# Attention and a token/channel mixer on one core: a relu of the weight narrowing put behind a copy of ys on ACT

## The chip, the cores and the metric

One NeuronCore of a Trainium2 chip runs the whole kernel in one launch. The metric is the device time of an execution in microseconds; lower is better. PE is the tensor engine (PEld its weight loads), DVE the vector engine, ACT the scalar engine, POOL the GpSimd engine, SP the engine that issues most DMAs. SPq, ACTq and so on are the engines' sequencers.

## The reference

```python
def _attn_ref(q, k, v):                      # (8, 8, 576, 64) each: batch, head, position, d
    q_s = softmax of q over d;  k_s = softmax of k over the 576 positions
    kv = np.einsum('bhsd,bhse->bhde', k_s, v)
    return np.einsum('bhsd,bhde->bhse', q_s, kv)

def reference(...):
    x = attn.transpose(0, 2, 1, 3).reshape(8, 576, 512)
    h = np.maximum(x.transpose(0, 2, 1) @ w_tok1, 0.0) @ w_tok2     # 576 -> 256 -> 576, over positions
    u = x + h.transpose(0, 2, 1)
    return u + np.maximum(u @ w_ch1, 0.0) @ w_ch2                   # 512 -> 1536 -> 512, over channels
```

The softmaxes are written out here in words. q, k and v come as fp32, the four weights as 64-bit floats.

## The kernel before, in words

**The units.** The attention and the token mixing are cut into 32 units of two heads each (128 channels by 576 positions). A unit goes through these stages: `softmax_k` (DVE maximum, ACT exponential `kt_t`) and `softmax_q` (DVE reductions and multiplications around an ACT exponential of `q_t`); `stage_qT` and `stage_kv` on PE (transposes of q and k through PSUM, the product `kvf` of k and v with its scale `rs`); `stage_y` (PE: q by w_tok1, then ACT copies the result out of PSUM as `ys`, L424); `stage_h1` (PE L430: `ys` by `kvf`, ACT relu to `hh`, DVE remainder to `hl`); `stage_u` (PE L464: `hh` and `hl` by w_tok2, added to the attention product; ACT casts the result to `uh`, DVE L472 writes the remainder `ul`). The pair hh/hl, uh/ul and so on is the high and low part of an fp32 number; products are taken as three passes of parts. The first 8 units are "early": they run while the weights are still being brought in. The other 24 run later, between the channel products.

**The weights.** A weight arrives as pairs of 32-bit words. `narrow` makes fp32 out of it in five DVE operations (L234, L236, L237, L239, L241) with one ACT relu (L235) behind the first of them; `split` then writes the high part with an ACT cast (L134) and the low part with a DVE subtraction (L135). `load_tok2` brings w_tok2 in this way as two pieces of 512 columns (n = 0 and 1) and a tail of 128. In the order lists cv_s_281 is the piece n = 1, ys_266 the ys of unit 0 and ys_359 that of unit 1.

**The rest.** The channel mixing runs over 9 groups of 512 positions: L487 makes a hidden block, L490 (ACT) and L491 (DVE) its relu in two parts `h`, L694 multiplies them by w_ch2. Groups 0 to 2 are done so, up to about 280 us. Meanwhile `keep_blocks` and `keep_sums` prepare sums of pairs of w_ch1 blocks for the groups after them: for each pair p, SP loads `whole` into the buffer stg (L516), DVE makes four sums (L518 to L521), ACT casts them (L134), DVE writes the remainder, and SP stores both to DRAM (L524, w<-stg). stg has two buffers, which every pair uses in turn. The groups 3 to 6 and then the last two together use these sums in a scheme of seven products per block pair.

**The order.** The program is written unit by unit, but a scheduler sets the order of each engine from a simulated timeline, so the written place of an instruction doesn't fix its place. Each engine takes its instructions strictly in the order that the scheduler wrote, and waits at the head of its line. `behind(list)` adds a constraint: instructions issued in its block come after the listed ones in the engine's order.

Of the kernel before, what the change touches and what calls it, by code (L numbers as in the profile page):

```python
# [11 lines left out]
AF = mybir.ActivationFunctionType  # L12
# [8 lines left out]
def attn_mixer_kernel(ctx: ExitStack, tc: tile.TileContext, q, k, kt, v, wt, out, dims):  # L21
# [3 lines left out]
    nc = tc.nc  # L25
    B, H, S, D, TOK, DM, DCH, wide = dims
# [47 lines left out]
    ebias = const.tile([P, 1], F32, name="ebias")  # L74
# [54 lines left out]
    def f32(ap):  # L129
        return ap.bitcast(F32)  # L130

    def split(hi, lo, src, lo_eng):

        nc.scalar.copy(hi, src)  # L134
        lo_eng.tensor_tensor(lo, src, f32(hi), op=ALU.subtract)  # L135
# [3 lines left out]
    def ps_unit(dtype=F32):  # L139

        pools = unit_banks[0]
        pool, name = pools[turn[0] % len(pools)]
        turn[0] += 1
        return pool.tile([P, 512], dtype, name=name)
# [7 lines left out]
    @contextmanager  # L152
    def behind(instructions):
        with ExitStack() as stack:
            for ins in instructions:
                stack.enter_context(tc.issue_after(ins))
            yield
# [32 lines left out]
    def load_weights(i, n=CW, out=None):  # L190

        if not wide:
            t = out if out is not None else cv.tile([P, C1 * P], F32, name="cv_s")[:, 0:n]
            nc.sync.dma_start(t, wt[i][:, 0:n])
            return t
        conv.append(conv.pop(0))
        raw = raw_tile(conv[-1][0])
        nc.sync.dma_start(raw[:, 0:n, :].rearrange("p n w -> p (n w)"), wt[i][:, 0:n].bitcast(U32))
        with behind(first):
            return narrow(raw, n, out)  # L200

    wide_pools = []
    spare = []

    def raw_tile(pool):
        if pool is not None:
            return pool.tile([P, CW, 2], U32, name="stg")
        if not spare:
            t = wide_pools[0].tile([P, 2 * CW, 2], U32, name="stg_w")
            spare.extend((t[:, 0:CW], t[:, CW : 2 * CW]))  # L210
        spare.append(spare.pop(0))
        return spare[-1]

    def load_wide(i, out=None):

        if not wide:
            t = out if out is not None else wide_pools[1].tile([P, 2 * CW], F32, name="cv_w")
            for x in range(2):
                nc.sync.dma_start(t[:, x * CW : (x + 1) * CW], wt[i + x])
            return t  # L220
        raw = wide_pools[0].tile([P, 2 * CW, 2], U32, name="stg_w")
        flat = raw.rearrange("p n w -> p (n w)")
        for x in range(2):
            nc.sync.dma_start(flat[:, x * 2 * CW : (x + 1) * 2 * CW], wt[i + x].bitcast(U32))
        with behind(first):
            return narrow(raw, 2 * CW, out, wide_pools[1].tile([P, 2 * CW], U32, name="cv_w"))

    def narrow(raw, n, out, s=None):


        w0, w1 = raw[:, 0:n, 0], raw[:, 0:n, 1]
        if s is None:
            s = conv[-1][1].tile([P, C1 * P], U32, name="cv_s")[:, 0:n]
        nc.vector.tensor_scalar(s, w1, 20, 0x7FF, op0=ALU.logical_shift_right, op1=ALU.bitwise_and)  # L234
        nc.scalar.activation(s, s, AF.Relu, bias=ebias, scale=2.0**23)  # L235
        nc.vector.scalar_tensor_tensor(s, w1, 0x80000000, s, op0=ALU.bitwise_and, op1=ALU.bitwise_or)  # L236
        nc.vector.tensor_scalar(w1, w1, 0xFFFFF, 0x100000, op0=ALU.bitwise_and, op1=ALU.bitwise_or)  # L237
        f1 = w1.bitcast(F32)
        nc.vector.scalar_tensor_tensor(f1, w0, 2.0**-32, w1, op0=ALU.mult, op1=ALU.add)  # L239
        z = s.bitcast(F32) if out is None else out  # L240
        nc.vector.tensor_tensor(z, f1, s.bitcast(F32), op=ALU.mult)  # L241
        return z
# [22 lines left out]
    def load_tok2():  # L265
        if WIDE2:
            t = load_wide(AT_T2).rearrange("p (n s) -> p n s", n=NT)
            split(w2h[:, :, 0:S0], w2l[:, :, 0:S0], t, nc.vector)
        else:
            for n in range(NT):  # L270
                split(w2h[:, n, 0:S0], w2l[:, n, 0:S0], load_weights(AT_T2 + n), nc.vector)
        t = load_weights(AT_TAIL + 1, NT * TL).rearrange("p (n t) -> p n t", n=NT)
        split(w2h[:, :, S0:S], w2l[:, :, S0:S], t, nc.vector)

    whole = {}

# [134 lines left out]
    def stage_y(u):  # L411
        y = ps_unit()
        if u["early"]:
            mm = [(u["q"][:, c, :], w1f[:, c, :]) for c in range(C1)]
        else:
            qh, ql = u["qh"], u["ql"]
            mm = []
            for c in range(C):
                mm += [(qh[:, c, :], w1h[:, c, :]), (qh[:, c, :], w1l[:, c, :]), (ql[:, c, :], w1h[:, c, :])]
            mm += [(qh[:, C, :], w1th), (qh[:, C, :], w1tl)]  # L420
        for i, (a, w) in enumerate(mm):
            nc.tensor.matmul(y[:, 0:TOK], a, w, start=(i == 0), stop=(i == len(mm) - 1))  # L422
        ys = (early if u["early"] else wk).tile([P, TOK], F32, name="ys")
        nc.scalar.copy(ys, y[:, 0:TOK])  # L424
        u["y"] = ys

    def stage_h1(u):
# [480 lines left out]
    units = {}  # L908
# [10 lines left out]
    def pe_stages(n):  # L919
        def s1():  # L920
            stage_qT(units[n])
            stage_kv(units[n])

        def s2():
            stage_y(units[n])

        def s3():
            stage_h1(units[n])

        def s4():  # L930
            stage_u(units[n], 0)

        def s5():
            stage_u(units[n], 1)

        return s1, s2, s3, s4, s5
# [27 lines left out]
    stages[0][1]()  # L964
    load_v(1)
    load_tok2()
    conv[:] = [(stg, cv)]
    for n in range(NE):
# [194 lines left out]
```

## Time and profile before

| what | us |
|---|---|
| median of three runs | 794.77 |
| the three runs | 794.04, 794.77, 797.56 |
| the profiled execution | 796.62 |
| its span | 794.8 |
| granted clock of PE, mean | 0.998 |
| busy: PE, PEld, DVE, ACT, POOL | 769.0, 670.9, 618.1, 341.9, 180.7 |

The profiled execution is one run of its own; it lies 1.85 above the median of the three, and 1.82 of its time lie outside the span. Busy times add up what an engine does; where two instructions of one engine overlap, the shorter of the stretches counts. In a timeline a row gives start and duration in us, the engine, the line, what it writes and reads, the shape, how many instructions the row holds, and in brackets the idle time before it and what ended that. Line numbers are those of the kernel before; the changed kernel's are 1 higher from L235 on and 3 higher from L276 on.

### The profile page before, as it was taken

The numbers are of one execution on the slowest core, as the hardware profiler recorded it, in microseconds if no ns is written. First come the engines' busy times: TensorE is split into PE (matmuls) and PEld (weight loads), VectorE is DVE, ScalarE is ACT, GpSimd is POOL, SyncE is SP. The second block draws the span as 40 slices with busy tenths as digits, with TensorE's granted clock in tenths as the row PEclk, the third lists the DMA queues.
The fourth block names the chain that finished last, engine by engine and source line by source line (L and its number), as shares of the span: only waits on it lengthen the run. The fifth ranks groups of instructions, "written<-read, shape, count | busy, mean of one in ns | idle before, by whom it ended". The sixth has DMA issues, their size and how long they took to land.

```text
span 794.8 us, 13455 instructions
## 1 busy us (share of the span) xinstructions
PE 769.0 (97%) x4824; PEld 670.9 (84%) x4824; DVE 618.1 (78%) x1101; ACT 341.9 (43%) x744; POOL 180.7 (23%) x130
## 2 busy tenths in 40 slices
PE   3899999999999999999999999999999999999998
PEld 2688888877888888899999999989999998888886
DVE  7979998978788874878688657888987557667971
ACT  4666433444454443434353334434444324346610
POOL 0000000011111352122211111232422320536640
PEclk9999999999999999999999999999999999999999
DMA  9655644158879785587879777999978543667776
GB/s 304 187 174 166 224 150 171 44 171 278 273 243 336 232 286 177 144 282 210 238 213 287 226 219 216 288 339 314 316 233 270 161 134 115 195 189 198 192 207 196
DMA packets 151459, 174.83 MB, mean 220 GB/s; under 512 B 51297, under 2 KB 98017, under 8 KB 151393
## 3 DMA queue, kind: packets, MB, share of 16 engines
q1 hardware_dynamic: 145056, 161.65, 67.2%
q10 hardware_dynamic: 6336, 12.32, 4.1%
q8 instruction: 38, 0.62, 0.3%
q14 instruction: 29, 0.23, 0.1%
HBM read 131.47 MB, written 42.47 MB: 219 GB/s over the span
## 4 chain that ended last, share of the span: by engine, by line
PE 70%; DVE 11%; issue 7%; DMA 7%; ACT 2%; POOL 1%; SPq 1%; DVEq 0%; POOLq 0%; ACTq 0%
PE ps_o L694 20%; PE ps_h L645 14%; PE ps_h L768 7%; PE ps_o L768 7%; PE ps_h L464 6%; PE ps_h L422 4%; PE ps_h L487 4%; PE ps_h L357 2%; DMA q_t<-in_q 2%; DMA stg<-whole 1%; PE ps_h L430 1%; PE ps_o L464 1%; PE ps_o L882 1%; DMA w<-stg 1%; DVE q_t L340 1%
## 5 line engine op out<-in xcount | busy, mean ns | idle before, releaser
L694 PE MATMUL ps_o<-h,c2h 128*128 128x512 f32 x544 | 184.2, 398 | 2.9 <-ACT h L490 1.9
L694 PEld LDWEIGHTS ps_o<-h,c2h 128*128 128x128 f32 x544 | 101.4, 188 | 23.8 <-ACT h L490 3.0
L694 PE MATMUL ps_o<-h,c2l 128*128 128x512 f32 x272 | 106.0, 393 | 0.0
L318 POOL TENSOR_TENSOR k_t<-k_t,dg 128x640 f32<-128x640 f32 x24 | 41.6, 1735 | 217.6 <-ACT dg L317 182.1
L135 POOL TENSOR_TENSOR ql<-q_t,qh 128x640 fp32r<-128x640 f32 x24 | 38.4, 1599 | 182.3 <-PE ps_o L694 104.2
L645 PE MATMUL ps_h<-th,ring 128*128 128x256 f32 x384 | 72.3, 283 | 0.0
L645 PEld LDWEIGHTS ps_h<-th,ring 128*128 128x128 f32 x384 | 60.1, 191 | 0.0
L694 PEld LDWEIGHTS ps_o<-h,c2l 128*128 128x128 f32 x272 | 51.3, 188 | 8.6
L487 PE MATMUL ps_h<-uh,c1l 128*128 128x512 f32 x144 | 56.2, 390 | 0.0
L487 PE MATMUL ps_h<-ul,c1h 128*128 128x512 f32 x144 | 56.2, 390 | 0.0
L487 PE MATMUL ps_h<-uh,c1h 128*128 128x512 f32 x144 | 56.1, 392 | 0.0
L645 PE MATMUL ps_h<-uh,ring 128*128 128x256 f32 x288 | 54.4, 282 | 0.6 <-DVE c L672 0.6
L645 PE MATMUL ps_h<-tl,ring 128*128 128x256 f32 x192 | 54.3, 283 | 0.0
L645 PEld LDWEIGHTS ps_h<-uh,ring 128*128 128x128 f32 x288 | 46.5, 190 | 2.8 <-DVE c L672 0.8
L471 ACT CAST uh<-ps_h 128x320 fp32r<-128x320 f32 (+4 forms) x76 | 24.4, 334 | 52.1 <-PE ps_h L464 32.1
L336 ACT ACTIVATE q_t<-q_t 128x640 f32<-128x640 f32 x32 | 23.6, 738 | 46.1 <-DVE q_t L327 43.1
L326 DVE TENSOR_REDUCE st<-q_t 128x10 f32<-128x640 f32 x32 | 26.1, 815 | 22.2 <-DMA q_t<-in_q 22.2
L490 ACT ACTIVATE h<-ps_h 128x512 fp32r<-128x512 f32 x36 | 21.5, 598 | 49.5 <-PE ps_h L487 42.0
L645 PE MATMUL ps_h<-ul,ring 128*128 128x256 f32 x144 | 40.6, 282 | 0.0
L645 PEld LDWEIGHTS ps_h<-tl,ring 128*128 128x128 f32 x192 | 36.8, 192 | 0.0
L472 DVE TENSOR_TENSOR ul<-ps_h,uh 128x320 fp32r<-128x320 f32 (+4 forms) x76 | 27.4, 370 | 9.0 <-ACT uh L471 8.8
L135 DVE TENSOR_TENSOR qtl<-q_t,qth 128x512 fp32r<-128x512 f32 (+1 forms) x48 | 25.6, 566 | 8.1 <-ACT qth L134 7.3
(319 smaller groups left out, 2070.2 us busy)
## 6 DMA issues: line engine op xcount, KB each, us to landing
ring<-w SPq DMA_DIRECT2D x210, 256.0 KB, 3.7
ring<-v SPq DMA_DIRECT2D x42, 256.0 KB, 3.0
kt_t<-in_kt SPq DMA_DIRECT2D x32, 320.0 KB, 3.7
q_t<-in_q SPq DMA_DIRECT2D x32, 320.0 KB, 3.7
v_t<-in_v SPq DMA_DIRECT2D x32, 320.0 KB, 4.5
stg_w<-in_w SPq DMA_DIRECT2D x18, 512.0 KB, 6.0
k_t<-in_k SPq DMA_DIRECT2D x24, 320.0 KB, 4.9
q<-cv_s SPq DMA_DIRECT2D x24, 320.0 KB, 3.2
```

The lines of the kernel that those rows point to most:

```text
L135: lo_eng.tensor_tensor(lo, src, f32(hi), op=ALU.subtract)
L318: nc.gpsimd.tensor_tensor(kx, kx, dg.unsqueeze(1).broadcast_to([P, C1, P]), op=ALU.subtract)
L326: nc.vector.tensor_reduce(st[:, 0, :], qt, axis=AX.X, op=ALU.max)
L336: nc.scalar.activation(qc, qc, AF.Exp)
L422: nc.tensor.matmul(y[:, 0:TOK], a, w, start=(i == 0), stop=(i == len(mm) - 1))
L464: nc.tensor.matmul(t[:, 0:N], a, w, start=(i == 0), stop=(i == len(mm) - 1))
L471: nc.scalar.copy(uh, src).ins,
L472: nc.vector.tensor_tensor(ul, src, f32(uh), op=ALU.subtract).ins,
L487: nc.tensor.matmul(t, a[:, n, :], w, start=(i == 0), stop=(i == 3 * NJ - 1))
L645: nc.tensor.matmul(t[:, cols], a, b[:, n], start=(i == 0), stop=(i == 5))
L694: m = nc.tensor.matmul(o, a[:, cs], w, start=(first and i == 0), stop=(last and i == 2))
L768: nc.tensor.matmul(o, a, b, start=first and i == 0 and (n == 0 or not one), stop=last and i == 2 and (n == 1 or not one))
```

## The change

`stage_y` keeps the instruction of the ys copy in the unit. While the second piece of w_tok2 (n = 1) and its tail are narrowed, the list `copied` holds the copy of unit 0, and the relu of `narrow` is issued behind it. For n = 0 and for all other weights the list is empty, and nothing is constrained.

```diff
-    spare = []
+    spare, copied = [], []
...
-        nc.scalar.activation(s, s, AF.Relu, bias=ebias, scale=2.0**23)
+        with behind(copied):
+            nc.scalar.activation(s, s, AF.Relu, bias=ebias, scale=2.0**23)
...
             for n in range(NT):
+                copied[:] = [units[0]["ys"]] if n else []
                 split(w2h[:, n, 0:S0], w2l[:, n, 0:S0], load_weights(AT_T2 + n), nc.vector)
         t = load_weights(AT_TAIL + 1, NT * TL).rearrange("p (n t) -> p n t", n=NT)
         split(w2h[:, :, S0:S], w2l[:, :, S0:S], t, nc.vector)
+        copied.clear()
...
-        nc.scalar.copy(ys, y[:, 0:TOK])
+        u["ys"] = nc.scalar.copy(ys, y[:, 0:TOK]).ins
```

The scheduler answers this with other choices behind it. No instruction is added or removed. Rows that differ run on PE from about row 49 to 850 of 3,200, on DVE from 68 to 400, on ACT from 25 to 260 and on SP from 29 to 97; POOL's list is the same, and so is everything from about 280 us on. Three places follow.

**First place: ACT in the head (about 28 to 32 us).** Before:

```order
L134 CAST w2h_104<-cv_s_270 128x512
L235 ACTIVATE cv_s_281<-cv_s_281,ebias_96 128x512
L424 COPY ys_266<-ps_h_260 128x256
L424 COPY ys_359<-ps_h_353 128x256
L303 ACTIVATE kt_t_390<-kt_t_390,mc_395 128x640
L437 ACTIVATE hh_364<-ps_o_361 128x256
L367 ACTIVATE kvf1_147<-ps_o_336,rs_348 64x64 x2
L303 ACTIVATE kt_t_480<-kt_t_480,mc_485 128x640
```

Now:

```order
L134 CAST w2h_104<-cv_s_270 128x512
L427 COPY ys_266<-ps_h_260 128x256
L236 ACTIVATE cv_s_281<-cv_s_281,ebias_96 128x512
L427 COPY ys_359<-ps_h_353 128x256
L306 ACTIVATE kt_t_390<-kt_t_390,mc_395 128x640
L440 ACTIVATE hh_364<-ps_o_361 128x256
L370 ACTIVATE kvf1_147<-ps_o_336,rs_348 64x64 x2
L306 ACTIVATE kt_t_480<-kt_t_480,mc_485 128x640
```

The relu of cv_s_281 and the copy of ys_266 have traded places; what stands behind them is the same.

**Second place: DVE at the softmax of the last early units (about 52 to 60 us).** st_820 and q_t_804 belong to the softmax of q of the last early unit, whose q is the transfer that DVE waits for there; the ul rows free the PSUM banks that PE writes next. Before:

```order
L472 TENSOR_TENSOR ul0_124<-ps_o_378,uh0_123 128x192
L326 TENSOR_REDUCE st_820<-q_t_804 128x10
L337 TENSOR_REDUCE st_704<-q_t_688 128x10
L327 TENSOR_TENSOR q_t_804<-q_t_804,st_820 128x640
L299 TENSOR_REDUCE mc_807<-kt_t_802 128x1
L472 TENSOR_TENSOR ul0_124<-ps_h_468,uh0_123 128x192
L472 TENSOR_TENSOR ul1_126<-ps_o_378,uh1_125 128x64
L472 TENSOR_TENSOR ul0_124<-ps_h_548,uh0_123 128x320
L338 TENSOR_SCALAR st_704<-st_704 128x10
L472 TENSOR_TENSOR ul0_124<-ps_o_558,uh0_123 128x192
```

Now:

```order
L475 TENSOR_TENSOR ul0_124<-ps_o_378,uh0_123 128x192
L340 TENSOR_REDUCE st_704<-q_t_688 128x10
L329 TENSOR_REDUCE st_820<-q_t_804 128x10
L341 TENSOR_SCALAR st_704<-st_704 128x10
L475 TENSOR_TENSOR ul0_124<-ps_h_468,uh0_123 128x192
L475 TENSOR_TENSOR ul1_126<-ps_o_378,uh1_125 128x64
L302 TENSOR_REDUCE mc_807<-kt_t_802 128x1
L475 TENSOR_TENSOR ul0_124<-ps_h_548,uh0_123 128x320
L475 TENSOR_TENSOR ul0_124<-ps_o_558,uh0_123 128x192
L330 TENSOR_TENSOR q_t_804<-q_t_804,st_820 128x640
```

Two of the ul rows now come ahead of the subtraction L330 and the maximum L302, and the sum reduction of st_704 ahead of the maximum that waits. A little further down on DVE stands hl_661, which PE needs for the next unit. Before:

```order
L234 TENSOR_SCALAR cv_w_573<-stg_w_570 128x1024
L234 TENSOR_SCALAR cv_w_587<-stg_w_584 128x1024
L338 TENSOR_SCALAR st_820<-st_820 128x10
L340 TENSOR_TENSOR q_t_688<-q_t_688,st_704 128x640
L438 SCALAR_TENSOR_TENSOR hl_661<-ps_h_657,hh_660 128x256
```

Now:

```order
L234 TENSOR_SCALAR cv_w_573<-stg_w_570 128x1024
L234 TENSOR_SCALAR cv_w_587<-stg_w_584 128x1024
L366 RECIPROCAL rs_644<-rs_644 128x1
L343 TENSOR_TENSOR q_t_688<-q_t_688,st_704 128x640
L340 TENSOR_REDUCE st_820<-q_t_804 128x10
L441 SCALAR_TENSOR_TENSOR hl_661<-ps_h_657,hh_660 128x256
```

The sum reduction of q_t_804 has come in ahead of hl_661.

**Third place: SP and DVE at the first pair sums (about 183 to 194 us).** stg_2029 and stg_2030 are the buffers of pair 0, w0_1955 its store in DRAM. SP before:

```order
L516 DMA stg_2029<-whole0_582 128x1024
L187 DMA v_t_91<-in_v 128x10x64
L178 DMA k_t_1876<-in_k 128x640
L507 DMA w0_1955<-c1h0_115 128x2x256
L508 DMA w0_1955<-c1h0_115 128x256
L165 DMA q_t_1874<-in_q 128x640
L507 DMA w0_1955<-c1l0_116 128x2x256
L508 DMA w0_1955<-c1l0_116 128x256
```

SP now:

```order
L187 DMA v_t_91<-in_v 128x10x64
L178 DMA k_t_1876<-in_k 128x640
L510 DMA w0_1955<-c1h0_115 128x2x256
L511 DMA w0_1955<-c1h0_115 128x256
L510 DMA w0_1955<-c1l0_116 128x2x256
L165 DMA q_t_1874<-in_q 128x640
L511 DMA w0_1955<-c1l0_116 128x256
L519 DMA stg_2029<-whole0_582 128x1024
```

The load of pair 0 has gone behind v, k, q and the four stores of w_ch1 blocks. DVE before:

```order
L518 TENSOR_TENSOR stg_2030<-stg_2029 128x256
L520 TENSOR_TENSOR stg_2030<-stg_2029 128x256
L339 RECIPROCAL st_1840<-st_1840 128x10
L519 TENSOR_TENSOR stg_2030<-stg_2030,stg_2029 128x256
L135 TENSOR_TENSOR kvl_1828<-kvf0_98,kvh_1827 128x128
L340 TENSOR_TENSOR q_t_1674<-q_t_1674,st_1840 128x640
L521 TENSOR_TENSOR stg_2030<-stg_2029,stg_2030 128x256
L299 TENSOR_REDUCE mc_2399<-kt_t_2238 128x1
L395 STREAM_TRANSPOSE cv_s_1974<-q_t_1674 128x5x4x32
L491 SCALAR_TENSOR_TENSOR h2_129<-ps_h_1857,h2_129 128x512
```

DVE now:

```order
L135 TENSOR_TENSOR kvl_1828<-kvf0_98,kvh_1827 128x128
L342 RECIPROCAL st_1840<-st_1840 128x10
L343 TENSOR_TENSOR q_t_1674<-q_t_1674,st_1840 128x640
L302 TENSOR_REDUCE mc_2399<-kt_t_2238 128x1
L398 STREAM_TRANSPOSE cv_s_1974<-q_t_1674 128x5x4x32
L494 SCALAR_TENSOR_TENSOR h2_129<-ps_h_1857,h2_129 128x512
L329 TENSOR_REDUCE st_2016<-q_t_1874 128x10
L330 TENSOR_TENSOR q_t_1874<-q_t_1874,st_2016 128x640
L521 TENSOR_TENSOR stg_2030<-stg_2029 128x256
L523 TENSOR_TENSOR stg_2030<-stg_2029 128x256
```

The remainder h2_129 of block ps_h_1857 has come ahead of the four pair sums. On ACT, the cast of pair 1 (stg_2212) stood ahead of two activations and then the relu L490 of ps_h_2040; now it stands behind those two, directly ahead of the relu.

## The prediction

> **What bounds the kernel now.** I read the busy line first, then the list of waits of the tensor engine (PE), then the windows around them, and last the timelines of the three places where the order of instructions changes beside a wait.
>
> ```profile
> span 794.8 us, 13455 instructions
> PE 769.0 (97%) x4824; PEld 670.9 (84%) x4824; DVE 618.1 (78%) x1101; ACT 341.9 (43%) x744; POOL 180.7 (23%) x130
> ```
>
> PE is busy for 769.0 of 794.8 us, so its idle time is only 25.8 us in all. A change that leaves PE's work alone can win no more than the part of this that it reaches.
>
> ```profile
> PE ps_o L694 <- ACT h L490: 1.9, 3, 1.0
> PE ps_o L430 <- ACT ys L424: 1.9, 1, 1.9
> ...
> PE ps_o L306 <- DVE ul L472: 1.1, 1, 1.1
> PE ps_o L694 <- DVE h L491: 1.0, 1, 1.0
> ...
> PE ps_h L309 <- DVE ul L472: 0.2, 1, 0.2
> ```
>
> Each row gives what PE waited for, total us, how many times, the longest. The wait for ys that the change names is the second one: one wait of 1.9 us.
>
> ```profile
> 20.00:30.00 10.00, 6.61 (x48) 4.85 (x47) 10.00 (x25) 6.27 (x13) 0.00 (x0) 1.00 0.81 237
> 30.00:31.00 1.00, 0.91 (x5) 0.85 (x6) 1.00 (x3) 1.00 (x4) 0.00 (x0) 0.84 0.94 260
> 31.00:32.00 1.00, 1.00 (x5) 0.73 (x4) 1.00 (x6) 0.96 (x5) 0.00 (x0) 0.50 0.70 265
> 34.00:35.00 1.00, 1.00 (x16) 0.74 (x14) 1.00 (x3) 0.29 (x1) 0.00 (x0) 0.95 0.76 253
> 28.00:280.00 252.00, 245.55 (x1432) 206.49 (x1432) 221.26 (x396) 123.93 (x264) 27.07 (x16) 0.99 0.64 204
> ```
>
> The columns are the window, its length, the busy time of PE, PEld, DVE, ACT and POOL, PE's granted clock, the share of DMA time and GB/s. From 20 to 30 us DVE is busy for all 10.00 us while PE is busy for 6.61: in the head DVE sets the pace. From 28 to 280 us, the stretch in which the two programs are ordered differently, PE is busy for 245.55 of 252.00 us. That leaves 6.45 us of idle time, the ceiling of what a new order can save, beside the clock: it is 0.50 from 31 to 34 us (the three windows read alike), and 0.84 and 0.95 in the windows at either end, about 3.4 us at half speed, 1.7 us of PE work at most.
>
> **Place A, the head (27 to 34 us).** Here the relu trades places with the copy of ys.
>
> ```profile
> 27.05 1.13 PE L422 MATMUL ps_h<-w1f,q_t 128*128 128x256 f32 x4
> 27.85 0.62 ACT L134 CAST w2h<-cv_s 128x512 fp32r<-128x512 f32 x1 [0.86 <-DVE cv_s L241]
> 28.60 0.42 DVE L234 TENSOR_SCALAR cv_s<-stg 128x512 uint32<-128x512 uint32 x1
> 29.06 0.72 ACT L235 ACTIVATE cv_s<-cv_s,ebias 128x512 uint32<-128x512 uint32 x1 [0.59 <-DVE cv_s L234]
> 29.68 0.62 ACT L424 COPY ys<-ps_h 128x256 f32<-128x256 f32 x2
> 30.09 0.71 PE L430 MATMUL ps_o<-kvf,ys 128*128 128x128 f32 x4 [1.91 <-ACT ys L424]
> 30.20 0.84 ACT L303 ACTIVATE kt_t<-kt_t,mc 128x640 f32<-128x640 f32 x1
> 30.99 0.16 DVE L363 RECIPROCAL rs<-rs 128x1 f32<-128x1 f32 x1
> 31.25 0.63 ACT L367 ACTIVATE kvf<-ps_o,rs 64x64 f32<-64x64 f32 x2
> 31.90 0.83 ACT L303 ACTIVATE kt_t<-kt_t,mc 128x640 f32<-128x640 f32 x1
> 33.50 0.94 PE L357 MATMUL ps_h<-v_t,k_t 128*64 128x65 f32 x16
> ```
>
> PE has finished the y product of unit 0 at 28.18 (27.05 + 1.13). ACT ends its cast at 28.47, then stands idle for 0.59 us: the relu waits for DVE L234, which ends at 29.02. Behind it the first ys is copied at 29.68. With the copy first it runs at 28.5 and takes some 0.4 us (the two copies together take 0.62, and PE starts 0.41 after the first begins), so PE starts L430 at about 28.9 instead of 30.09. The relu starts at 29.06 or little later, since it still waits for DVE; nothing is lost there, and its followers on DVE (L236 comes at 31.12) have 1.3 us to spare. So the named wait goes nearly whole. But PE stands in line for the next thing: its next products need the exponentials L303, which come after the copies on ACT. The first one can start at most the 0.3 us earlier that ACT wins by filling its 0.59 us gap with work. Then ACT meets L367, which waits for the reciprocal on DVE (30.99 to 31.15), and DVE has no gap to give. So L367 stays at 31.25, the second L303 at 31.9, and L357 at 33.50. Of 1.9 us, then, I count −0.2; the bounds are 0 and −1.91 (the wait, if nothing came up behind it), and I stay near the first as the row of L367 pins it.
>
> The clock: here PE was idle for 1.91 us and the next windows are at 0.50 for about 3.4 us. [...] Whether the fall comes at all when the idle time is moved and cut into pieces no run here shows. If it doesn't, the next microseconds hold up to 1.7 us less PE time. I give that a rival of its own below, and nothing in the sum.
>
> **Place B (52 to 61 us).** DVE waits for a transfer of q; now the ul parts come straight behind the reduction that it waits for.
>
> ```profile
> 52.68 0.82 DVE L326 TENSOR_REDUCE st<-q_t 128x10 f32<-128x640 f32 x1 [3.07 <-DMA q_t<-in_q]
> 55.81 0.21 DVE L472 TENSOR_TENSOR ul<-ps_o,uh 128x64 fp32r<-128x64 f32 x1
> 56.08 0.66 PE L306 MATMUL ps_o<-ident,kt_t 128*128 128x128 f32 x4 [1.12 <-DVE ul L472]
> 57.80 0.33 PE L309 MATMUL ps_h<-ident,kt_t 128*128 128x128 f32 x1 [0.19 <-DVE ul L472]
> 57.93 1.28 DVE L234 TENSOR_SCALAR cv_w<-stg_w 128x1024 uint32<-128x1024 uint32 x2
> 59.94 0.41 DVE L438 SCALAR_TENSOR_TENSOR hl<-ps_h,hh 128x256 fp32r<-128x256 f32 x1
> 60.88 0.54 PE L464 MATMUL ps_o<-w2h,hl 128*128 128x320 f32 x2
> ```
>
> Before, a sum reduction, a subtraction and a maximum stand between L326 and the ul that frees the PSUM bank (52.68 to 55.81). After, only a small scalar operation and one ul do, so the bank is free at about 53.9 and both waits, 1.12 + 0.19 = 1.31, go. But the product of w2h and hl, which PE reached at 60.88 without a wait, then comes up at about 58.9, while hl is still behind the two L234 (1.28 together), a multiplication and a reduction. hl starts at 59.2 if DVE runs without a gap, and at 59.8 with the small waits that it has now, against 59.94. PE then waits for hl for 0.8 to 1.3 us. PE does some things (L430) afterwards instead of before, 0.7 us of work, so the gain left at this point is 0 to 0.5. I take −0.2. The bounds are −1.31 (no new wait) and +1 (hl 1 us late, if the exponential that the reduction needs is late too).
>
> **Place C and D (183 to 210 us), pair sums of the channel weights.**
>
> ```profile
> 183.53 0.34 SPq L516 DMA_DIRECT2D stg<-whole  x1
> 188.99 0.47 SPq L508 DMA_DIRECT2D w<-c1l  x1
> 189.38 0.42 DVE L518 TENSOR_TENSOR stg<-stg 128x256 f32<-128x256 f32 x1 [1.75 <-DMA stg<-whole]
> 193.87 1.20 PE L694 MATMUL ps_o<-h,c2h 128*128 128x512 f32 x4 [1.00 <-DVE h L491]
> 197.25 0.33 SPq L516 DMA_DIRECT2D stg<-whole  x1
> 206.50 1.05 ACT L134 CAST stg<-stg 128x1024 fp32r<-128x1024 f32 x1 [1.34 <-DVE stg L521]
> 208.50 0.60 ACT L490 ACTIVATE h<-ps_h 128x512 fp32r<-128x512 f32 x1
> 209.15 0.50 PE L694 MATMUL ps_o<-h,c2h 128*128 128x512 f32 x1 [0.22 <-ACT h L490]
> ```
>
> ```profile
> 236.61 3.36 DMA w<-stg
> 254.53 4.98 DMA stg<-whole
> ```
>
> The first fence is the timeline, the second the chain that ended last (start, duration, what).
>
> C: L518 of pair 0 waits for its load for 1.75 us at the head of DVE's line; behind it comes L491, for which PE waits 1.00 us at 193.87. In the new order L491 is ahead of the four sums. So C is −1.0 (bounds −1.0 and 0).
>
> D: on SP the load of pair 0 (183.53) now stands behind v, k, q and the four w stores, the last of which is issued at 188.99. These move up by its 0.43 us, so the load is issued at about 189.0, 5.5 us late. Nobody waits for the sums themselves at once, but pair 1 uses the same buffers. Pair 0's data land 5.2 us later (between 4.98 and the 5.85 from 183.53 to 189.38; I take a value near the first, as the loads queued ahead are now gone), at 194.2; four sums of about 0.35 us, a cast of 1.05 and the store of 3.36 put pair 1's load at about 200.0 to 200.7, against 197.25. The same steps put pair 1's cast at 206.6 to 207.3 at best, about 207.3 with its start on a busy DVE. In ACT's new order this cast stands directly ahead of L490, whose h PE needs at 209.15; before, it had two activations behind it. The cast ends at 208.35, L490 takes 0.60 plus 0.05 to PE: PE starts at 209.0. Without this it would be there at 208.93 − 1.4 (A, B and C) = 207.53. So PE waits 1.47 in place of 0.22: D is +1.25, with bounds −0.2 (the cast is early) and +6 (it carries its 5.5 us through).
>
> The two other waits for L490 (1.9 in three, of which this was 0.2) have the same neighbours in both orders and stay. From 63 to 160 us I followed the new order row by row with the old durations and found no wait that isn't in the old one; the store of a narrowed channel weight is the tight place there. From 280 us the two programs have the same order, so what is won or lost by then is passed on.
>
> **The sum.** −0.2 − 0.2 − 1.0 + 1.25 = −0.15 us. The profiled execution took 796.62, its span 794.8; it would be 796.5. It lies 1.85 above the median of the three runs, so against that median, 794.77, I forecast 794.6. PE's idle time changes place more than it shrinks.
>
> **The rivals.**
> 1. The freed time is kept. B brings no new wait for hl and the cast of pair 1 comes early. Then A −0.3, B −1.31, C −1.0, D −0.2: −2.8, so 792.0. For it speaks that DVE idles for 3.07 us ahead of 52.68 and so isn't short of time there; against it, that hl is written within 0.7 us of the old time by the sum of DVE's durations alone.
> 2. Slower: the chain of the pair sums carries its 5.5 us through to the cast of pair 1, which stands ahead of L490. The cast then starts at 206.50 + 5.5 = 212.0, ends at 213.05, and PE starts at 213.7, 4.55 after 209.15: about 799.3. It decides from the point where the cast starts after 207.5; each microsecond later is one lost. For it speaks the 1.34 us for which this cast already waits for DVE; against it, that the old chain holds pauses between the sums (189.38 to the second load at 197.25) which the new order needn't keep.
> 3. The clock doesn't fall to 0.50 at 31 us. That is worth up to 1.7 us of PE time, less about 0.3 that DVE's pace takes back as in A; with the sum of −0.15, 793.2. [...]
> 4. Something in the hundreds of moved rows that I haven't foreseen, such as the tight weight store: either sign, several us.
>
> **How the numbers follow.** I give 0.48 to the forecast (own range 793.0 to 796.8), 0.17 to rival 1, 0.08 to rival 3, 0.14 to rival 2 and 0.13 to rival 4. One half of one per cent, about what a measurement of this kernel can tell from no change, is 4.0 us: 790.8 to 798.7. Faster than this needs more than half of the 6.45 us: 0.12 (half of rival 4 and the tails of 1 and 3). Slower: 0.17, most of rival 2 and the other half of rival 4. The rest, 0.71, lies within. The range takes in rivals 1 and 3 with a margin and reaches to rival 2: 790.0 to 799.5.
>
> **What would show it.** Right: the 1.9 us wait for ys at 30.09 gone, L430 at about 28.9, but a PE wait for L303 or L306 behind it, and L357 still at 33.3 to 33.5; no wait for ul at 56, but one for hl of about 1 us near 60; no wait for L491 near 193, but one for L490 of 1 to 2 us near 209, directly behind the cast of stg. Wrong: L357 a microsecond earlier (DVE wasn't the bound there); the second load of whole before 198 or after 203; new waits of PE between 63 and 160, above all for a narrowed weight; a clock below 1.00 anywhere but at 31 us.

## The result, and the profile after

| | kernel before | changed kernel |
|---|---|---|
| median, us (runs) | 795.27 (6) | 801.10 (6) |
| lowest to highest | 794.00 to 797.56 | 799.09 to 802.27 |
| profiled execution, span | 796.62, 794.8 | 799.89, 798.1 |

The ratio is 1.0081 with a 95% interval of 1.0057 to 1.0105: the change costs 5.8 us at the median, 3.3 us between the two profiled executions. No change had been forecast (794.6, range 790.0 to 799.5).

The page of the changed kernel, its busy line:

```profile
span 798.1 us, 13460 instructions
PE 771.3 (97%) x4824; PEld 672.3 (84%) x4824; DVE 619.6 (78%) x1101; ACT 342.0 (43%) x744; POOL 180.2 (23%) x130
```

PE's work is the same 4,824 instructions; its idle time is 26.8 us against 25.8, and the other 2.3 us of the 3.3 are longer busy time for the same work. The list of waits of PE in the changed kernel (us, times, longest) says where:

```profile
PE ps_o L697 <- ACT h L493: 4.9, 3, 2.7
...
PE ps_h L433 <- ACT kvf L370: 0.9, 1, 0.9
PE ps_h L490 <- DVE c1l L135: 0.6, 1, 0.6
PE ps_h L467 <- DVE h L494: 0.5, 1, 0.5
```

The waits for ys and for ul are gone. The three waits for the relu of h (L490 before, L493 now) have grown from 1.9 to 4.9. The timeline of PE shows the pieces, with the idle time and what ended it in brackets:

```profile
31.35 0.66 PE L309 MATMUL ps_h<-ident,kt_t 128*128 128x128 f32 x4 [0.47 <-ACT kt_t L306]
...
76.89 0.71 PE L433 MATMUL ps_h<-kvf,ys 128*128 128x128 f32 x4 [0.88 <-ACT kvf L370]
...
137.42 0.50 PE L490 MATMUL ps_h<-uh,c1l 128*128 128x512 f32 x1 [0.59 <-DVE c1l L135]
...
166.00 0.56 PE L697 MATMUL ps_o<-h,c2h 128*128 128x512 f32 x1 [2.69 <-ACT h L493]
...
211.24 0.50 PE L697 MATMUL ps_o<-h,c2h 128*128 128x512 f32 x1 [1.97 <-ACT h L493]
```

The one at 166 stood at 165.02 before and was 0.96 long:

```profile
165.02 0.50 PE L694 MATMUL ps_o<-h,c2h 128*128 128x512 f32 x1 [0.96 <-ACT h L490]
```

Behind it, in the changed kernel, the clock is down (windows of 1 us; the third column from the end):

```profile
166.00:167.00 1.00, 1.00 (x3) 0.83 (x4) 1.00 (x3) 0.15 (x1) 0.00 (x0) 0.65 0.00 0
167.00:168.00 1.00, 1.00 (x3) 0.77 (x3) 1.00 (x3) 0.46 (x1) 0.00 (x0) 0.50 0.71 133
168.00:169.00 1.00, 1.00 (x4) 0.74 (x3) 1.00 (x4) 0.00 (x0) 0.00 (x0) 0.50 0.99 352
169.00:170.00 1.00, 1.00 (x6) 0.83 (x5) 0.55 (x1) 0.00 (x0) 0.00 (x0) 0.65 0.28 105
```

That is 3.4 us at half speed (0.7 + 1 + 1 + 0.7), as much as before at 31 us, where the changed kernel now reads 1.00 throughout.

In this profile the wait for ys went for another reason than the swap. A row of PE before, then a row of PE, one of ACT and a window of the changed kernel:

```profile
22.70 0.66 PE L306 MATMUL ps_o<-ident,kt_t 128*128 128x128 f32 x4 [1.57 <-ACT kt_t L303]
```

```profile
22.69 1.12 PE L309 MATMUL ps_o<-ident,kt_t 128*128 128x128 f32 x4 [1.02 <-ACT kt_t L306]
29.31 0.37 ACT L427 COPY ys<-ps_h 128x256 f32<-128x256 f32 x1 [0.85 <-PE ps_h L425]
22.00:24.00 2.00, 1.31 (x6) 1.31 (x7) 2.00 (x5) 1.52 (x3) 0.00 (x0) 1.00 0.61 226
```

The same four products take 1.12 us instead of 0.66. In the kernel before, the same four of another unit take 1.06 where the clock is down (31.45), so they took as long here as at a granted clock of 0.50, although this window reads 1.00. PE ended the y product of unit 0 at 29.7 instead of 28.18, and the copy waited 0.85 us for PE.

To follow the lead of one program over the other I compared the starts of the 36 relus L490 one by one. The changed kernel is 1.85 us ahead of the one before at the first (84.53 against 86.38), still 0.74 ahead at 155.73, behind by 1.97 at 175.01, and by 2.6 to 2.9 from 270 us on. So 4.7 us were lost between the first relu and 270 us. The lead of 1.85 is no measure of the change: late, mid, seg107 and sp_only (below), whose order is that of before up to 83 us, begin the first of these relus at 83.87 to 85.98.

The place near 161 us in the two kernels, first before, then changed, on POOL and DVE:

```profile
160.70 0.43 DVE L234 TENSOR_SCALAR cv_s<-stg 128x512 uint32<-128x512 uint32 x1 [0.93 <-DMA stg<-in_w]
161.00 1.57 POOL L318 TENSOR_TENSOR k_t<-k_t,dg 128x640 f32<-128x640 f32 x1 [13.03 <-ACT dg L317]
```

```profile
160.25 1.57 POOL L321 TENSOR_TENSOR k_t<-k_t,dg 128x640 f32<-128x640 f32 x1 [12.73 <-ACT dg L320]
161.09 1.02 DVE L234 TENSOR_SCALAR cv_s<-stg 128x512 uint32<-128x512 uint32 x1 [1.16 <-DMA stg<-in_w]
```

PE and with it POOL's addition come 0.75 us earlier, the raw weights 0.39 later. Before, DVE's first step of narrowing (L234) led POOL's addition by 0.30 us and took 0.43; now it begins under the addition and takes 1.02. The relu of the same weights waits for it, and further on in ACT's line stands the relu of h that PE waits for. The wait grew by 1.73 us: 0.75 because PE came earlier, 0.39 because the data came later, 0.59 because L234 took longer. The last two make the 0.98 us by which PE starts later than before.

And the narrowing of the weights ahead of that, SP and DVE in the changed kernel:

```profile
85.64 8.51 SPq L173 DMA_DIRECT2D kt_t<-in_kt  x2
95.48 1.76 SPq L224 DMA_DIRECT2D stg_w<-in_w  x4
```

```profile
93.70 1.23 DVE L242 TENSOR_TENSOR cv_w<-stg_w,cv_w 128x1024 f32<-128x1024 f32 x1
...
101.22 0.69 DVE L234 TENSOR_SCALAR cv_w<-stg_w 128x1024 uint32<-128x1024 uint32 x1 [0.96 <-DMA stg_w<-in_w]
```

And before:

```profile
92.88 2.04 SPq L224 DMA_DIRECT2D stg_w<-in_w  x4
98.63 0.68 DVE L234 TENSOR_SCALAR cv_w<-stg_w 128x1024 uint32<-128x1024 uint32 x1
```

The last step of the piece ahead (L242, before L241) began at 93.70 instead of 90.11. PE was 1.85 us ahead at 85 us; the weights were 2.6 behind.

### The profile page after: what moved, and what is told of

It reads as the page before. It is cut to its first block, busy times and chain, and to the rows that moved or that the text cites. A ratio compares the mean times of both kernels' runs of the same rounds, so it can differ in the third digit from the quotient of the medians.

```text
span 798.1 us, 13460 instructions
## 1 busy us (share of the span) xinstructions
PE 771.3 (97%) x4824; PEld 672.3 (84%) x4824; DVE 619.6 (78%) x1101; ACT 342.0 (43%) x744; POOL 180.2 (23%) x130
## 4 chain that ended last, share of the span: by engine, by line
PE 73%; DVE 14%; DMA 8%; ACT 2%; issue 1%; SPq 1%; POOL 0%; DVEq 0%; ACTq 0%; POOLq 0%
PE ps_o L697 22%; PE ps_h L648 15%; PE ps_h L771 7%; PE ps_h L467 7%; PE ps_o L771 6%; PE ps_h L490 5%; PE ps_h L425 5%; DMA stg_w<-in_w 3%; PE ps_h L360 2%; DVE stg_w L240 1%; PE ps_h L433 1%; DVE cv_w L237 1%; DMA w<-c1h 1%; PE ps_o L885 1%; DVE q_t L343 1%
## 5 line engine op out<-in xcount | busy, mean ns | idle before, releaser
L490 PE MATMUL ps_h<-uh,c1l 128*128 128x512 f32 x144 | 56.3, 391 | 0.6 <-DVE c1l L135 0.6
L490 PE MATMUL ps_h<-ul,c1h 128*128 128x512 f32 x144 | 56.1, 390 | 0.0
L490 PE MATMUL ps_h<-uh,c1h 128*128 128x512 f32 x144 | 56.1, 391 | 0.0
L493 ACT ACTIVATE h<-ps_h 128x512 fp32r<-128x512 f32 x36 | 21.5, 598 | 45.4 <-PE ps_h L490 33.1
```

The costliest lines, as they stand in the source:

```text
L490: nc.tensor.matmul(t, a[:, n, :], w, start=(i == 0), stop=(i == 3 * NJ - 1))
```

## The experiments

**How they are made.** One constraint had moved hundreds of rows, so the parts had to be separated. Each kernel here is the source of the kernel before with the order of PE, DVE, ACT and SP up to about 280 us written down and held; the rows in which the two kernels differ fall into separate stretches, and each kernel takes some stretches from the changed kernel and the others from before. Their lines are those of the kernel before. None holds the order of the kernel before unaltered, so what the holding itself does to the time is not measured.

```diff
+def pin_order(tc):
+    traced = {i.name: i for i in tc.nc.cur_bb.bb.instructions}
+    info = mybir.DependencyInfo(mybir.DependencyClass.NoSync, mybir.DependencyReason.DATA)
+    for names in ORDER.values():            # per engine, a list of instructions
+        names = ["I-" + x for x in names.split()]
+        for x, y in zip(names, names[1:]):
+            tc.add_manual_dep(traced[y], x, info, reason="order")
...
     both_groups()
+    pin_order(tc)
```

| kernel | taken from the changed kernel (number of the instruction on its engine) | ratio to before | interval | PE's wait near 165: until, us, cause | clock behind it |
|---|---|---|---|---|---|
| before | nothing | 1 | | 165.02, 0.96, L490 | 1.00 |
| changed | all | 1.0081 | 1.0057 to 1.0105 | 166.00, 2.69, L490 | falls |
| s_only | ACT 26, 27: the swap | 0.9964 | 0.9947 to 0.9982 | 163.28, 1.00, L490 | 1.00 |
| head60 | PE to 257, DVE to 133, ACT to 97 | 0.9988 | 0.9971 to 1.0004 | 163.33, 2.69, L490 | 1.00 |
| early80 | PE to 303, DVE to 158, ACT to 115, SP to 46 | 1.0022 | 1.0002 to 1.0043 | 165.61, 2.69, L490 | falls |
| early | PE to 699, DVE to 259, ACT to 179, SP to 59 | 1.0059 | 1.0036 to 1.0083 | 168.22, 3.57, L490 | falls |
| late | all behind early's | 1.0018 | 0.9994 to 1.0041 | 164.69, 1.03, L490 | 1.00 |
| seg66 | PE 258 to 303, DVE 134 to 158, ACT 98 to 115, SP 30 to 46 | 1.0090 | 1.0057 to 1.0123 | 165.28, 1.24, L490 | 1.00 |
| mid | PE 304 to 379, DVE 159 to 195, ACT 116 to 134, SP 47 to 54 | 1.0039 | 1.0017 to 1.0061 | 165.38, 2.69, L490 | falls |
| seg107 | PE 380 to 699, DVE 196 to 259, ACT 135 to 179 | 1.0077 | 1.0050 to 1.0105 | 167.67, 2.78, L490 | falls |
| minus_mid | all but mid's | 1.0094 | 1.0062 to 1.0126 | 168.38, 2.68, L490 | falls |
| no_swap | all but ACT 26, 27 | 1.0101 | 1.0067 to 1.0134 | 166.16, 2.93, L490 | falls |
| sp_only | SP 47 to 51 | 1.0077 | 1.0050 to 1.0103 | 168.79, 2.69, L490 | falls |
| after_sp | all but SP 47 to 51 | 1.0173 | 1.0136 to 1.0210 | 173.11, 2.69, L490 | 1.00 |
| h_first | head60's, and one block's L490, L491 forward | 1.0033 | 1.0011 to 1.0056 | 165.01, 2.13, c1h L134 | falls |
| head60_dg | head60's, and a swap on ACT | 1.0011 | 0.9989 to 1.0032 | 164.91, 2.74, L490 | 1.00 |
| early80_dg | early80's, and the same swap | 1.0065 | 1.0049 to 1.0080 | 164.91, 2.87, L490 | falls |
| s_only_dg | s_only's, and the same swap | 1.0036 | 1.0021 to 1.0051 | 164.66, 2.41, L490 | falls |

Each was timed in five rounds beside the kernel before. That kernel's own median was 793.85 to 796.40 us from session to session, so kernels of different sessions are compared by their ratios. The last two columns are of the one profiled execution.

**The swap alone.**

```diff
 L134 CAST w2h_104<-cv_s_270 128x512
-L235 ACTIVATE cv_s_281<-cv_s_281,ebias_96 128x512
 L424 COPY ys_266<-ps_h_260 128x256
+L235 ACTIVATE cv_s_281<-cv_s_281,ebias_96 128x512
```

> The order of every engine is held to that of the kernel before; only the relu of cv_s_281 and the copy of ys_266 trade places on ACT. Theory 1 (what is gained ahead of the weights is taken back at 166 us, where the narrowing of the last weights sets the time): the head wins 0.5 to 1.9 us on PE by 85 us, the wait for L490 near 165 grows by as much (0.96 to between 1.5 and 2.9), and the time stays within 1 us of before, or becomes up to 1.5 slower if that wait makes the clock fall. Rival (the swap itself pays, the reordering behind it costs): 1 to 2.5 us faster than before, and the wait near 165 stays about 1 us.

It is 0.36% faster than the kernel before: 2.27 us at the median, as the rival had it, and the longer wait near 165 of theory 1 didn't come. The timeline and two windows of its profile:

```profile
28.89 0.71 PE L430 MATMUL ps_o<-kvf,ys 128*128 128x128 f32 x4 [0.61 <-ACT ys L424]
30.92 0.66 PE L306 MATMUL ps_h<-ident,kt_t 128*128 128x128 f32 x4 [0.88 <-ACT kt_t L303]
```

```profile
28.00:32.00 4.00, 2.50 (x17) 1.71 (x15) 4.00 (x13) 3.44 (x8) 0.00 (x0) 1.00 0.85 284
32.00:36.00 4.00, 4.00 (x35) 3.19 (x34) 4.00 (x10) 2.65 (x7) 0.00 (x0) 1.00 0.39 112
```

PE's 1.91 us in one piece have become 0.61 and 0.88 in two, and the clock stays at 1.00. Everything behind, the narrowing of the weights too, comes 1.7 us earlier, and the wait near 165 (163.28) keeps its size, 1.00.

**The stretches.**

> The changed kernel's order on all engines up to about 66 us (swap, first two early units' PE and DVE rows, the ul rows near 55 us), the order before from there on. Theory 1: PE is 1.5 to 2.5 us ahead of before by 85 us, and waits 2.5 to 3.2 us instead of 0.96 for L490 near 165; time -0.5 to +1.5 against before. Rival (nothing takes it back, the cost lies in the rows from 66 us on): 1.5 to 3 us faster.

> The changed kernel's order on all engines up to about 160 us (swap, early units, narrowing of the channel weights), the order before from there on. Theory 1 with the clock: the wait near 166 of about 2.7 us and the half clock behind it as in the changed kernel, so 1.0 to 2.5 us slower than before at 181 us; the one at 193 still there (1.0), none of 2 us near 210; in all 1 to 3 us slower than before. Rival (all of the loss comes from the pair sums): 1 to 2 us faster.

> The order before up to about 160 us, the changed kernel's from there on (the loads of the pair sums behind the stores of w, the cast of pair 1 ahead of L490). Rival 2 of the prediction (the pair sums carry their delay to L490): wait for L490 near 210 of 1.5 to 2.5 us in place of 0.22, that of 1.0 near 193 gone, so +0.5 to +1.5 by 215 us, and 1 to 3 us slower in all with the small waits near 252 and 275. If all of the loss came from the pair sums: +5 us.

head60 does what theory 1 says of the wait: the waits for ul near 56 us are gone as well, PE stands at the wait for L490 earlier (2.69), and starts again at 163.33, where s_only started at 163.28. Its time, 0.94 us less than before, lies in neither range. early makes most of the loss, 5.0 us where I had expected 1 to 3, with the wait at 3.57 us and the clock down behind it; its rival (all from the pair sums) is out. late costs 0.18%, not clear of nothing, and its wait near 208 is 1.00 us, less than expected.

> The order of the kernel before on every engine, but on SP the load of kt_t_1672 stands ahead of the loads of stg_w_1031 and stg_w_1045 (raw weights), as in the changed kernel; no swap on ACT. Theory 2 (this one place on SP makes the narrowing of the last channel weights about 5 us late, since SP waits at that load until the buffer of kt_t is free): the raw loads are issued 3 to 6 us later than in the kernel before, DVE L234 of cv_w_1034 starts 2.5 to 5.5 us later, PE's wait for L490 near 166 grows from about 1 to 2.5 to 4.5; 2.5 to 5.5 us slower than before. Rival (the order of DVE among the narrowings costs it, SP's doesn't): within 1 us of before.

> The changed kernel's order on every engine, but on SP the loads of stg_w_1031 and stg_w_1045 stand ahead of that of kt_t_1672 again, as before. Theory 2: the raw loads are issued near 90 us, the narrowing comes 2 to 5 us earlier than in the changed kernel, the wait near 166 falls to 1 to 2.7; 3 to 5.5 us faster than the changed kernel, so -1 to +2.5 against before, with the pair sums' cost left in it. Rival: within 1.5 us of the changed kernel, +4.5 to +6.5 against before.

```diff
 L173 DMA kt_t_1521<-in_kt 128x640
+L173 DMA kt_t_1672<-in_kt 128x640
 L224 DMA stg_w_1031<-in_w 128x1024 x2
 L224 DMA stg_w_1045<-in_w 128x1024 x2
-L173 DMA kt_t_1672<-in_kt 128x640
```

That is sp_only's edit; after_sp is its reverse in the changed kernel. sp_only, DVE and SP:

```profile
101.77 0.69 DVE L234 TENSOR_SCALAR cv_w<-stg_w 128x1024 uint32<-128x1024 uint32 x1 [4.30 <-DMA stg_w<-in_w]
```

```profile
88.05 6.58 SPq L173 DMA_DIRECT2D kt_t<-in_kt  x2
94.75 2.08 SPq L224 DMA_DIRECT2D stg_w<-in_w  x4
```

One transposition on SP costs 6 us, somewhat more than theory 2 gave it: SP is at two loads of kt_t for 6.58 us (88.05 to 94.63), the raw weights go out at 94.75, and DVE idles for 4.30 us. But theory 2 fell with after_sp, which I had expected 3 to 5.5 us faster than the changed kernel and which came out 5 slower by the medians and 7 by the ratios:

```profile
104.15 0.75 DVE L299 TENSOR_REDUCE mc<-kt_t 128x1 f32<-128x576 f32 x1 [7.08 <-DMA kt_t<-in_kt]
...
107.36 0.69 DVE L234 TENSOR_SCALAR cv_w<-stg_w 128x1024 uint32<-128x1024 uint32 x1
```

The changed order of DVE has the maximum of kt_t (L299) ahead of L234. With kt_t loaded last, DVE stands at it for 7.08 us. And the raw loads still go out at 95.17, since in this order of DVE their buffer is read late (L241, 93.80 to 95.02). Each engine's order was made for the others'; here, putting back one alone is worse than either.

> The changed kernel's order on every engine, but the relu of cv_s_281 stands ahead of the copy of ys_266 again. Theory 1 (what the head wins is taken back where PE waits for the last weights, which SP and DVE set): the clock falls near 31 us again and PE is 1 to 2 us later at 85 us, but the time is within 1 us of the changed kernel, +5 to +7 against before. Rival (the swap's gain of 2 us is kept whatever follows): 1.5 to 2.5 us slower than the changed kernel, +7.5 to +9 against before.

This run doesn't decide. By the medians the time stays that of the changed kernel (801.74 against 801.10), as theory 1 has it. Against the kernel before in its own session it is 7.9 us slower, which is the rival's figure (+7.5 to +9), and the two intervals overlap. In its profile the clock did not fall in the head (1.00 in every window up to 38 us), and the first relu L490 came at 83.74, 0.79 ahead of the changed kernel, so the profile doesn't show what it costs to take the swap out.

> The order of head60 (the changed kernel's up to about 66 us, before's from there on), with one more move: the two halves of the hidden block of ps_h_1588 (L490 on ACT, L491 on DVE) come ahead of the narrowing of the last weights, directly behind L235 and L236 of cv_s_1452. Theory 1: the wait for L490 near 163 (2.69 in head60) falls to 0.3 to 1.0, and 1 to 2 us are won on head60, 2 to 4 us on the kernel before. Rival (the last weights set the time, whoever comes first on ACT): PE waits for c1 or c2 of block 10 or 11 a few us later instead, and the time is that of head60 within 0.7 us.

```diff
 L235 ACTIVATE cv_s_1452<-cv_s_1452,ebias_96 128x512
+L490 ACTIVATE h2_129<-ps_h_1588 128x512
 L367 ACTIVATE kvf0_98<-ps_h_1617,rs_1629 64x64 x2
...
 L235 ACTIVATE cv_s_1464<-cv_s_1464,ebias_96 128x512
-L490 ACTIVATE h2_129<-ps_h_1588 128x512
```

The rival was right about the wait: PE no longer waits for h, but 2.13 us for the weights themselves. The time is worse than head60's (1.0033 against 0.9988), which neither had.

```profile
165.01 0.79 PE L487 MATMUL ps_h<-uh,c1h 128*128 128x512 f32 x1 [2.13 <-ACT c1h L134]
```

> The changed kernel's order on all engines up to about 83 us, the order before from there on. Theory 3 (the loss is made between 83 and 107 us, where on DVE the last step of narrowing cv_w_793, L241, goes behind the split of w1 and on SP the raw loads behind kt_t_1672, each enough by itself to make the next weights late): the raw loads of cv_w_1034 issued near 90 to 92 us, L234 of cv_w_1034 at 95 to 98, PE's wait for L490 near 165 between 1 and 2.7; -2.5 to +1 against before. Rival (the loss is made earlier, by the load of stg_w_776 behind that of v_t at 65 us): +3 to +6.

> The order before everywhere, but the changed kernel's in the stretch from about 83 to 107 us on DVE, ACT, SP and PE. Theory 3: L241 of cv_w_793 near 95, the raw loads issued near 95 to 98, L234 of cv_w_1034 2.5 to 5 us later than before; +3 to +7 against before, nearly the whole loss. Rival (the loss is spread over the narrowings from 107 to 160 us): within 1.5 us of before.

> The changed kernel's order everywhere, but the order before in the stretch from about 83 to 107 us on DVE, ACT, SP and PE (the counterpart of mid). Theory 3: 3 to 6 us faster than the changed kernel, -1 to +2.5 against before; what is left of the loss is the pair sums' wait near 210. Rival: within 2 us of the changed kernel.

> The order before everywhere, but the changed kernel's in the stretch from about 66 to 83 us on DVE, ACT, SP and PE (among it the load of stg_w_776 behind that of v_t on SP). Theory 4 (the loss is not made at one place: each stretch between 66 and 160 us makes the narrowing of the last weights later, and PE's wait near 165 collects it): +1 to +3.5 against before, the wait for L490 near 165 between 1.5 and 2.7. Rival (this stretch costs only behind the changed head): within 1 us of before.

> The order before everywhere, but the changed kernel's in the stretch from about 107 to 160 us on DVE, ACT and PE. Theory 4: the raw loads of the last weights (L198) issued 2 to 7 us later near 130 us, a wait near 165 of 2 to 3.5; +1.5 to +5 against before. Rival (the loss is made before 107 us alone): within 1 us of before.

Theory 3 (one place, 83 to 107 us) fell: mid alone costs 0.39%, less than expected, and the changed kernel without it is as slow as with it. early80, at 2.0 us over before, lies between theory 3 and its rival. Theory 4 held in its sign: seg66, mid and seg107 each cost by themselves, seg66 and seg107 (6.4 and 6.5 us) more than I had given them. But they don't add up: 0.90, 0.39 and 0.77% alone, 0.59% together in early. seg107's profile shows the raw load (L198) that before is issued at 127.32 issued at 134.42, 7.1 us later; in seg66's it is only 2 late, its wait near 165 is 1.24, not the 1.5 to 2.7 expected, and its profiled execution is one of its two fastest (797.36, its median is 800.84), so that what its others lost isn't shown.

**The collision.** That small slips cost as much alone as together pointed to a threshold, and the profiles have one. Where DVE's L234 of cv_s_1452 begins ahead of POOL's L318 (before by 0.30 us, late 0.23, s_only 0.25, seg66 0.02), it takes 0.43 us and PE's wait is 0.96 to 1.24. Where it begins behind, in ten profiles, it takes 1.02 to 1.81, ends 0.28 to 0.29 us after L318, and the wait is 2.68 to 3.57. In seven of the ten the wait is 2.68 or 2.69 and PE starts 5.74 or 5.75 us after L318 does, whether L234 began 0.05 us behind it (head60) or 0.84 (the changed kernel): beyond the threshold the size of the slip, 0.05 to 0.84 us, no longer counted here. In the other three (early, seg107, no_swap) the next L234 also waited 0.58 to 1.37 us for its data. In head60:

```profile
157.59 1.57 POOL L318 TENSOR_TENSOR k_t<-k_t,dg 128x640 f32<-128x640 f32 x1 [12.77 <-ACT dg L317]
157.64 1.81 DVE L234 TENSOR_SCALAR cv_s<-stg 128x512 uint32<-128x512 uint32 x1 [1.08 <-DMA stg<-in_w]
```

Three kernels hold POOL's addition back, by putting the copy that it waits for behind the relu of cv_s_1452:

```diff
+L235 ACTIVATE cv_s_1452<-cv_s_1452,ebias_96 128x512
 L317 COPY dg_1640<-ps_h_1642 128x128
-L235 ACTIVATE cv_s_1452<-cv_s_1452,ebias_96 128x512
```

> head60 with one swap on ACT: the copy dg_1640 (L317), for which POOL's addition L318 waits, comes behind the relu L235 of cv_s_1452 instead of ahead of it. Theory 5 (DVE's L234 of cv_s_1452 takes 0.43 us alone, but until the end of POOL's L318 when that has begun first; before, it began 0.30 us ahead of L318): L318 now begins behind the relu, L234 takes about 0.43 instead of 1.81, PE's wait for L490 near 163 falls from 2.69 to between 0.9 and 1.5; 0.8 to 2 us faster than head60. Rival (the long L234 is only a late landing of its data, POOL has no part in it): L234 still ends near 159.4, the wait stays 2.7, the time is that of head60 within 0.7.

> early80 with the same swap of dg_1640 and the relu of cv_s_1452 on ACT. Theory 5: L234 takes 0.43 instead of 1.67, the wait near 165.6 falls from 2.69 to between 1.1 and 1.7, the clock falls there less often; 1 to 3 us faster than early80, 0 to 1.5 faster than the kernel before. Rival: the wait stays 2.7 and the time is that of early80 within 0.7.

> s_only with the same swap of dg_1640 and the relu of cv_s_1452 on ACT. Here L234 already ran ahead of L318, so theory 5 expects little: L234 0.43 as before, L236 0.69 instead of 1.13 at most, the wait near 163 between 0.6 and 1.1; within 0.7 of s_only. Rival (the swap helps by letting the relu go first, not by keeping POOL off): 1 us faster than s_only or more.

The collision is real, its removal no gain: theory 5 had all three faster or the same, and each is slower than the kernel it was made from (1.0011 against 0.9988, 1.0065 against 1.0022, 1.0036 against 0.9964). The rows of head60_dg on DVE, POOL and ACT:

```profile
159.18 0.43 DVE L234 TENSOR_SCALAR cv_s<-stg 128x512 uint32<-128x512 uint32 x1 [1.08 <-DMA stg<-in_w]
160.65 1.91 POOL L318 TENSOR_TENSOR k_t<-k_t,dg 128x640 f32<-128x640 f32 x1 [14.28 <-ACT dg L317]
161.44 1.41 DVE L234 TENSOR_SCALAR cv_s<-stg 128x512 uint32<-128x512 uint32 x1 [0.29 <-DMA stg<-in_w]
162.59 0.74 ACT L319 ACTIVATE k_t<-k_t 128x640 f32<-128x640 f32 x1 [1.16 <-POOL k_t L318]
```

L234, with the same wait for its data ahead of it, takes 0.43 instead of 1.81, against the rival (a late landing). But L318 now runs later, the next L234 falls under it (1.41), and ACT's L319, which stands ahead of L490, waits for L318: PE's wait is 2.74 again. In s_only_dg, which had no collision to lose, the same swap makes one at the next L234 (1.60) and turns the wait of 1.00 into 2.41. So what the wait is made of is shown: the relu of h stands behind both the narrowing and POOL's addition, and got through early only in the four profiles where the two fell as before. How much of the time this wait makes is not shown: head60 has it at 2.69 and is not slower than before, and seg66 is 0.90% slower with 1.24 in its profile.

## Why the prediction was wrong

**A, the head: the swap's size about right, the path and the clock wrong.** The wait for ys went, but in the changed kernel's profile because PE came late to it, which is luck; a shorter one for kt_t came (0.47), as said. I had L357 pinned at 33.3 to 33.5 by ACT's L367 and the second L303. These two came 0.20 later than before (31.45 and 32.10), and yet L360 (L357 before) began at 32.48: they didn't pin it. Counted from PE's first product of kt_t behind 21 us (L306, 22.70 before), L357 follows after 9.53 us with the relu first and no fall of the clock (seg66, no_swap), after 9.24 or 9.25 with the copy first (nine profiles), and after 10.30 to 10.80 with the relu first and a fall near 31 us (before, late, seg107, sp_only). So the swap itself is worth 0.28 us here, near the −0.2 of the sum, and the fall costs 0.8 to 1.3. That the fall stays away was rival 3; the 0.08 that I gave it was my guess, with nothing behind it but the fall in the one profile of before. What decides whether the clock falls isn't shown. It fell behind 1.91 us without PE work in the head of the kernel before and behind 2.69 near 166 in the changed one, for about 3.4 us each time; in seg66 and no_swap, with 1.92 and 1.91 us at the same place in the head, it stayed at 1.00.

**B: the gain was right, the wait that was to take it back didn't come.** Both waits for ul are gone. hl was written at 56.19 and PE used it at 57.15 without a wait; I had put hl at 59.2 to 59.8, counting DVE's rows from 52.68, where it waited for q; in the changed kernel that row begins at 49.75. The load of that q went out 1.28 us earlier (44.55 against 45.83); the rest of the 2.93 us isn't shown.

**C: right.** No wait for L491 near 193.

**D: right in its chain, too small.** The load of pair 1 went out at 202.37 (forecast 200.0 to 200.7), its cast began at 209.64 (207.3), PE started at 211.24 (209.0) after 1.97 us (1.47). The changed kernel was already 1.97 us late at 175.01, so not all of this lateness is D's. By itself the stretch costs little: late, 1.0018, with a wait of 1.00 there.

**The step that failed** is the one I took in two sentences: "I followed the new order row by row with the old durations and found no wait that isn't in the old one", and the two other waits for L490 "have the same neighbours in both orders and stay". The neighbours are the same; the wait is not a property of neighbours. It is the difference of two times, PE's arrival and the arrival of weights that SP, DVE and POOL bring, and the change moved both, apart: PE earlier, the weights later. The order up to about 160 us costs 0.59% by itself (early), where the sum had −0.4 us from A and B and nothing more. Of the sum's missing terms the profile shows the wait at 166 (2.69 instead of 0.96), about 3.4 us of half clock behind it, and 0.88 and 0.59 us of new waits at 76.89 and 137.42. Rival 2 had the right side with the wrong place; rival 4, "something in the hundreds of moved rows", named the tight weights, and had 0.13.

Which part of the loss each of these makes stays open: the wait near 165 and the time don't go together from kernel to kernel. The gap between 3.3 us (profiled executions) and 5.8 (medians) is not explained either; the executions of one kernel spread over 2 to 10 us.

## What to carry to other kernels

A constraint given to a scheduler is not a swap: to know what a swap is worth, hold the rest of the order. Here the swap alone was 0.36% faster and the reordering that it set off cost more than 1% (1.0081 over 0.9964). When PE is moved ahead, look at the next place where it waits for something that other engines bring, and at the margins there, not at its neighbours: here a margin of 0.30 us between a DVE and a POOL instruction was used up, and the wait behind them went from 0.96 to 2.69. A granted clock of 1.00 in a window should be checked against how long the same products take elsewhere: here four products took 1.12 us in one kernel and 0.66 in the other, and the windows of both (22 to 24 us) read 1.00. And an order of one engine should be put back only together with the others': four loads moved back on SP alone made the changed kernel 5 to 7 us slower.

## What the runs showed of the hardware

A DVE operation of one tensor and scalars on 128x512 words (L234 of cv_s_1452) took 0.43 us where it began ahead of POOL's addition, and 1.02 to 1.81 where it began under an addition of 1.56 or 1.57 us: it ended 0.28 to 0.29 us after POOL did, in all ten profiles where the two met so. Which of the two began first made the difference: with L234 ahead by 0.30 us (before) it kept its 0.43 and POOL's addition its 1.57, and with L234 ahead by only 0.02 (seg66) it kept its 0.43 and POOL's addition took 1.85. What the two engines share there, no run shows.

The granted clock fell at a PE wait of 2.1 to 3.6 us near 165 us in 11 of 14 profiles (mean clock of those executions 0.994 to 0.998), and not at one of 1.24 or less in the four others. Of the three of the 14 in which it didn't fall, head60 and after_sp have a mean clock of 1.0. It was down for 3.4 us in the changed kernel (0.65, 0.50, 0.50, 0.65), and in seg107, early80_dg and s_only_dg the windows of 5 us behind the wait (0.78 and 0.88, 0.66, 0.66) come to the same 3.4 us at a clock of one half. In the head (about 31 us), with the relu first and one wait of 1.9 us for ys, a fall came near 31 us in four of six profiles (0.50 from 31 to 34 us in before); with the copy first and two waits of 0.6 and 0.9, in none of nine. In the three others PE was slower near 23 us (four products of one unit took 1.06 us at 23.82 in the changed kernel and in head60_dg, against 0.60 before; in mid the clock read 0.50 from 24 to 26 us), came later to ys and waited 0.47 once; no fall near 31 followed. So where a wait of 1.9 us was cut in two, more than the 0.28 us that the swap itself gave in the head could be won: a fall cost 0.8 to 1.3. The granted clock didn't show every slow stretch: in the changed kernel four products of one unit take 1.06 to 1.12 us up to 23.82 and 0.60 to 0.66 from 31.35 on, and the windows of both read 1.00.
